# Key loads into five common buffers, four score buffers, four products ahead of their quads, and filler matmuls in the next operation's bank

## The chip, the cores and the metric

The kernel runs on one NeuronCore of a Trainium2 chip, in one launch. The metric is the device time of that core in microseconds, the median of several executions. Five engines run their own instruction streams and wait for each other through semaphores: TensorE (PE in the profile, its weight loads PEld), VectorE (DVE), ScalarE (ACT), GpSimd (POOL) and SyncE (SP), which here issues all DMA transfers.

## The reference

Attention over pooled keys and values, then a two-layer network with an unusual activation, all in fp32:

```python
# q, k, v: 8 batches x 8 heads x 576 positions x 64
k_p = k.reshape(B, H, Sp, pool, D).mean(axis=3)      # pool = 8, Sp = 72
v_p = v.reshape(B, H, Sp, pool, D).mean(axis=3)
scores = scale * np.matmul(q, k_p.transpose(0, 1, 3, 2))
attn = np.exp(scores - max); attn = attn / (sum + 1e-09)
x = np.matmul(attn, v_p)                             # as 4608 tokens x 512
h = x @ w_in                                         # 512 -> 2048
g = h * erf(softplus(h))
out = g @ w_out                                      # 2048 -> 512
```

## The kernel before

**Tiling.** The 4608 tokens are cut into nine chunks of 512. Chunk 0 goes through both matrix products directly (`plain_in`, then `second`). The other eight chunks are taken in four pairs. For a pair the first product is done by Strassen's scheme in Winograd's form: seven half-size products in place of eight. Sums and differences of the tokens' halves (`sides`: T1 to T4, B11 to B22) and of the weights' blocks (`sums`: S1 to S4) are made on DVE and POOL. Each fp32 operand is split into a high and a low part (`halves`; in the profile `x`, `w`, `ws`, `gl`), and a product is three matmuls for each 128 rows of the contraction (`three`), so that one product of the first layer is six matmuls of 128x512. The second layer of pairs 2 to 4 uses the same scheme (`seconds`), that of pair 1 doesn't.

**A quad.** `quad(s, i, ...)` makes eight of these per pair, each with the products S2·T2, S3·T3, S1·T1, A12·B21, A22·T4 and S4·B22, and A11·B11 unless that was made before. DVE adds them up as they come: v = p1 + S2T2, u = v + S3T3, g11 = u + S1T1, g00 = p1 + A12B21, then g10 and g01 (L831). A22·T4 accumulates onto the bank that S3·T3 used, so it can start only when u has been added; S4·B22 goes onto the bank of S1·T1 and needs g11. In pair 1 the first `HEADS = 7` quads have A11·B11 (p1) made ahead by `head`, between the second product of chunk 0 and the quads.

**The tokens come from attention.** `job` handles up to 256 positions of a batch. It loads keys and values (`load_pool`, a DMA each and one DVE reduction over 8), copies the pooled keys into `kbd`, then per tile of 128 positions: scores on PE (L579), maximum on DVE, exponentials on ACT (chunk 0: 8 instructions a tile with their sums, L598), normalisation, transposes on PE (L631, L634), values on PE (L674, L675), and x from the `att` banks. Keys land in `raw`, two buffers of their own of 128x576; the scores `s`, with their maxima `m` and sums `z`, have two buffers each, `bb` one.

**Who sets the order.** Every operation is recorded as an `Op` with a cost, a priority and the buffers that it holds. `Program.once` is a list scheduler over these with planned durations; `order` runs it eight times with new priorities and keeps the shortest plan. Each engine then executes its instructions in the planned order. A buffer kind has a number of places (`CAPS`), and most kinds share `PLACES` tiles of 128x512 in SBUF (`u`). The eight PSUM banks are shared by the kinds `h`, `o`, `att` and `cv`.

**Fillers.** Until the planned time `FILL` (57,000 ns) one bank is kept for filler matmuls (bf16, 128x256, on the constants; L998 in the profile): where the plan has PE idle ahead of an operation, as many of them are put there as fit into that idle time less `MARGIN`. After `FILL` there are none, and the bank goes to the other kinds.

Of the kernel before, what the change touches and what calls it, by code (L numbers as in the profile page):

```python
# [20 lines left out]
POOL = 8  # L21
# [4 lines left out]
P = 128  # L26
# [21 lines left out]
ON_DVE = 8  # L48
STORE = 6
HEADS = 7  # L50
EARLY, READY = (0, 0, 20, 32, 32), 14
ON_ACT = (0,)
CAPS = {"g": 32, "x": 28, "xr": 11, "w": 14, "ws": 10, "w0": 36, "gl": 12, "t": 6, "f": 3, "q": 2, "q0": 4, "f0": 14, "v": 3, "vm": 1, "low": 2, "sw": 8,
        "h": 6, "o": 4, "att": 4, "cv": 2, "dl": 3, "p1": 8}
SLACK, SLACK_SP, BIAS = 30, 400, 2000
FILL, MARGIN = 57000.0, 300
# [3 lines left out]
PLACES = 87  # L60
# [68 lines left out]
class Program:  # L129
# [100 lines left out]
    def once(self):  # L230
# [16 lines left out]
        spare = None  # L247
        if self.filler:
            spare = heapq.heappop(slots["bank"])
            self.idle.place = spare[1]  # L250
        for _ in self.ops:
# [100 lines left out]
def moe_attention(ctx: ExitStack, tc: tile.TileContext, cst, qa, kl, vl, wi, wo, out):  # L352
# [13 lines left out]
    sizes = {"u": PLACES, "bank": 8, "raw": 2, "et": 1, "etb": 1, "s": 2, "m": 2, "z": 2, "bb": 1, "ks": 1, "vs": 1, "d": 5}  # L366
# [148 lines left out]
    def job(ck, b, tiles, off, times, first, fresh):  # L515

        base, due, whole = times[0], times[-1] + VAL_R, ck > 2
        if fresh:
            ks, vs = buf("ks", [NP, SP]), buf("vs", [NP + 2, D])

            on_dve = b < ON_DVE

            def load_pool(src, dst, p, size, prio, tag):
                shape = [size, POOL] if on_dve else [POOL, size]
                t = buf("raw", shape) if tag == "raw" else place("v", F32, shape)
                op("SP", 15 * size, prio - 1, lambda: nc.sync.dma_start(
                    t.ap, src.rearrange("(p a b) -> p a b", p=P, b=t.ap.shape[2])), [], [t])
                if on_dve:
                    op("DVE", dve(8 * size), prio, lambda: nc.vector.tensor_reduce(  # L529
                        dst.ap[:, p, :], t.ap, AX.X, ALU.add), [t], [(dst, p)])  # L530
                else:
                    op("POOL", gps(4 * size), prio, lambda: nc.gpsimd.tensor_add(
                        t.ap[:, 0:4], t.ap[:, 0:4], t.ap[:, 4:8]), [t], [t])
                    op("POOL", gps(2 * size), prio, lambda: nc.gpsimd.tensor_add(
                        t.ap[:, 0:2], t.ap[:, 0:2], t.ap[:, 2:4]), [t], [t])
                    op("POOL", gps(size), prio, lambda: nc.gpsimd.tensor_add(
                        dst.ap[:, p, :], t.ap[:, 0], t.ap[:, 1]), [t], [(dst, p)])
# [7 lines left out]
            for p in range(NP + 2):  # L545
                load_pool(vl[b, p], vs, p, D, base + VALS + VALS_R * p,
                          "v")
# [263 lines left out]
    def quad(s, i, x, base, p1=None):  # L811
# [23 lines left out]
        g = {(m, t): place("g") for m in range(2) for t in range(2)}  # L835
# [161 lines left out]
    pr.idle = idle  # L997
    pr.filler = Op("PE", 107, 0, lambda: nc.tensor.matmul(  # L998
        idle.ap[:, :256], cb[:, :P], cb[:, :256], start=True, stop=True))
# [41 lines left out]
```

## Time and profile before

| | us |
|---|---|
| runs | 871.18, 877.29, 869.67 |
| median | 871.18 |
| the profiled execution | 870.09 |
| its span (first to last instruction) | 868.3 |
| granted TensorE clock, mean of the span | 0.996 |

The profiled execution lies 1.8 us above its own span and 1.1 us below the median. The profile names an instruction by line, engine, operation and the tiles it writes and reads (`h<-x,w` is a product of the first layer, `o<-gl,w` one of the second). In the timeline view a row is a run of equal instructions: start, duration from the first start to the last end, count, and in brackets the idle time of that engine before it with what ended it. In the windows view a row is a stretch of time with each engine's busy time, then the granted TensorE clock, the share of the DMA engines' time and the rate. Matmuls overlap, so six of them that take 1.52 us from first start to last end follow each other every 1.36 us.

### The profile page before, as it was taken

How to read it: one execution, taken by the hardware profiler on the slowest of the kernel's cores; microseconds unless marked ns; L12 is line 12 of the kernel's file. 1: busy time of each engine (PE TensorE's matmuls, PEld its weight loads, DVE VectorE, ACT ScalarE, POOL GpSimd, SP SyncE). 2: the span in 40 equal slices, each digit the busy share in tenths (PEclk: the TensorE clock that was granted, in tenths of full speed). 3: DMA queues.
4: the chain of work that ended last, by engine and by line, in shares of the span. 5: the costliest groups of instructions: out<-in, count | busy, mean ns of one | idle time of the engine just before them, and what ended most of it. 6: DMA issues, size and time to landing. Idle time of an engine off the chain costs nothing.

```text
span 868.3 us, 13644 instructions
## 1 busy us (share of the span) xinstructions
PE 850.9 (98%) x4134; PEld 702.7 (81%) x4134; DVE 698.6 (80%) x1272; ACT 574.4 (66%) x989; POOL 459.9 (53%) x482
## 2 busy tenths in 40 slices
PE   8999999799999999999999999999999999999998
PEld 7787788687888888888888888887887888888886
DVE  4987898989887888688798997877879975767872
ACT  4889877569884455478985642978866446777640
POOL 2888697567786774065557352564474323442310
PEclk9999999989999999999999999999999999999999
DMA  8899999997999899885285578924753679447541
GB/s 307 312 307 342 303 402 332 324 359 266 295 316 349 331 348 311 314 317 174 85 303 160 163 257 275 362 86 134 224 152 109 219 254 340 126 131 256 190 157 50
DMA packets 125208, 218.04 MB, mean 251 GB/s; under 512 B 16976, under 2 KB 31440, under 8 KB 125136
## 3 DMA queue, kind: packets, MB, share of 16 engines
q1 hardware_dynamic: 125136, 217.18, 72.6%
q8 instruction: 33, 0.54, 0.2%
q14 instruction: 39, 0.32, 0.1%
HBM read 167.84 MB, written 49.28 MB: 250 GB/s over the span
## 4 chain that ended last, share of the span: by engine, by line
PE 72%; DVE 2%; issue 0%; ACT 0%; DVEq 0%
PE o L746 36%; PE h L746 29%; PE att L579 3%; PE att L674 3%; PE att L631 1%; PE att L675 1%; DVE g L766 0%; DVE gl L411 0%; PE att L634 0%; DVE g L894 0%; DVE g L831 0%; DVE f L918 0%; DVE ks L529 0%; DVE t L831 0%; DVE s L624 0%
## 5 line engine op out<-in xcount | busy, mean ns | idle before, releaser
L746 PE MATMUL o<-gl,w 128*128 128x512 f32 x1584 | 377.1, 393 | 0.5 <-DVE g L769 0.3
L746 PEld LDWEIGHTS o<-gl,w 128*128 128x128 f32 x1584 | 292.7, 188 | 61.9 <-DVE gl L411 0.9
L746 PE MATMUL h<-x,w 128*128 128x512 f32 x1344 | 316.9, 392 | 2.0 <-DVE t L831 1.2
L746 PEld LDWEIGHTS h<-x,w 128*128 128x128 f32 x1344 | 249.7, 188 | 55.8 <-DVE t L831 2.5
L766 POOL TENSOR_TENSOR g<-d,g 128x512 f32<-128x512 f32 x68 | 90.7, 1351 | 98.7 <-ACT d L762 75.8
L399 ACT ACTIVATE gl<-g 128x512 fp32r<-128x512 f32 x185 | 109.3, 625 | 46.2 <-DVE g L894 20.2
L411 POOL TENSOR_TENSOR gl<-g,gl 128x512 fp32r<-128x512 f32 x67 | 100.0, 1501 | 66.8 <-ACT gl L399 32.4
L411 DVE TENSOR_TENSOR gl<-g,gl 128x512 fp32r<-128x512 f32 x149 | 110.2, 767 | 6.2 <-POOL gl L400 3.9
L831 DVE TENSOR_TENSOR g<-t,h 128x512 f32<-128x512 f32 x96 | 65.5, 684 | 31.6 <-PE h L746 29.9
L758 ACT ACT_TABLE_LOAD x48 | 61.6, 1283 | 20.7 <-PE h L746 20.0
L762 ACT ACTIVATE d<-d 128x1024 f32<-128x1024 f32 x72 | 73.7, 1054 | 0.4
L894 POOL TENSOR_TENSOR g<-g 128x512 f32<-128x512 f32 x36 | 51.8, 1439 | 25.0 <-DVE g L894 19.3
L758 ACT ACTIVATE d<-g 128x512 f32<-128x512 f32 x103 | 59.1, 623 | 5.6 <-DVE g L831 5.4
L831 DVE TENSOR_TENSOR t<-t,h 128x512 f32<-128x512 f32 x57 | 39.0, 685 | 27.8 <-PE h L746 26.1
L746 PE MATMUL h<-x,ws 128*128 128x512 f32 x192 | 48.4, 407 | 4.5 <-POOL sw L496 2.9
L762 ACT ACT_TABLE_LOAD x40 | 51.3, 1283 | 0.7
L399 ACT ACTIVATE x<-xr 128x512 fp32r<-128x512 f32 (+2 forms) x60 | 32.5, 563 | 28.9 <-DVE xr L720 21.5
L746 PEld LDWEIGHTS h<-x,ws 128*128 128x128 f32 x192 | 38.0, 199 | 13.1 <-POOL sw L496 3.0
L674 PE MATMUL att<-et,va 128*128 128x256 f32 (+3 forms) x192 | 45.5, 339 | 2.0 <-DVE s L604 1.4
L579 PE MATMUL att<-kbd,q 128*128 128x144 f32 (+1 forms) x320 | 45.9, 287 | 0.4 <-DVE x L694 0.4
L579 PEld LDWEIGHTS att<-kbd,q 128*128 128x128 f32 (+1 forms) x320 | 42.3, 179 | 5.0 <-issue 1.6
L642 ACT COPY et<-att 128x512 f32<-128x512 f32 (+1 forms) x40 | 21.8, 544 | 34.5 <-PE att L631 33.5
(91 smaller groups left out, 1145.3 us busy)
## 6 DMA issues: line engine op xcount, KB each, us to landing
w<-ws SPq DMA_DIRECT2D x192, 256.0 KB, 4.5
w<-wo SPq DMA_DIRECT2D x136, 256.0 KB, 3.6
w<-wi SPq DMA_DIRECT2D x96, 256.0 KB, 5.0
ws<-ws SPq DMA_DIRECT2D x64, 256.0 KB, 4.0
v<-vl SPq DMA_DIRECT2D x48, 256.0 KB, 5.7
raw<-kl SPq DMA_DIRECT2D x32, 288.0 KB, 4.5
out<-f SPq DMA_DIRECT2D x36, 256.0 KB, 2.0
q<-qa SPq DMA_DIRECT2D x32, 256.0 KB, 5.2
```

The source lines that it names most:

```text
L399: op("ACT", act(n), prio, lambda: nc.scalar.activation(dst(), src(), AF.Copy, scale=scale), *access, turn=turn, alt=("POOL", 0.833 * n + 1 ...
L411: both(True, dve(n), gps(n), prio + 0.1, lambda e: e.tensor_sub(lo(), src(), f32(hi())), reads + [hikey], [lokey])
L579: nc.tensor.matmul(o, raw.ap[:, p, :T], kbd[:, p], start=(p % 2 == 0), stop=True, skip_group_check=True)
L631: nc.tensor.transpose(pa.ap[:, P * p:P * p + T], sp[:, p, 0:P], ident[:T, :T])
L642: op("ACT", act(4 * T, True), r + 2.3, lambda: nc.scalar.copy(et.ap[:, :, cs], pav()), [pa], [(et, k)])
L674: nc.tensor.matmul(o, va[:, p], et.ap[:, p, :n], start=e == 0, stop=False, skip_group_check=True)
L746: nc.tensor.matmul(o, u, v, start=first and q == 0, stop=last and q == 2, skip_group_check=True)
L758: nc.scalar.activation(y(k), hs[k][0].ap, AF.Softplus)
L762: op("ACT", act(1024), prio + 0.2, lambda k=k: nc.scalar.activation(ys[k].ap, ys[k].ap, AF.Erf), own[2 * k:2 * k + 2], own[2 * k:2 * k + 2 ...
L766: both(True, dve(512), gps(512), prio + 0.3, lambda e, k=k, h=h: e.tensor_mul(h.ap, y(k), h.ap), [own[k], h], [h])
L831: op("DVE", dve(512), prio, lambda: nc.vector.tensor_add(dst.ap, u.ap, o.ap), [u, o], [dst])
L894: both(True, dve(512), gps(512), prio, lambda e: e.tensor_sub(out.ap, u.ap, v.ap), [u, v], [out])
```

## The change

**Keys.** `load_pool` is written anew. A batch's keys come as four blocks of 128x512 (64 of the 72 pooled positions of each head pair) and a fifth of 128x256 with the remaining 8 positions of all four pairs, and land in kind `k`: at most five of the common places, in place of the two `raw` buffers. That is 40 key transfers and 40 reductions in place of 32. The host lays keys and values out accordingly. All pooling was on DVE before (`ON_DVE` was 8 of 8 batches) and still is.

**Score buffers.** `s`, `m` and `z` have four buffers, `bb` has two. `PLACES` goes from 87 to 88, and an unused pad shrinks.

**Necks.** `neck` makes A12·B21 and its addition g00 = p1 + A12B21 for the first `NECKS = 4` quads of pair 1, after the heads. These quads then leave both out and take g00 as it is.

**Fillers.** No bank is kept. A filler writes the bank that the next operation takes anyway, so it stands only ahead of an operation that takes a new bank, and only from the planned time at which that bank is free. Besides the time until `FILL`, an idle time of more than `LONG_IDLE` (1,200 ns of the plan) is filled later too.

```diff
-ON_DVE = 8
-HEADS = 7
+HEADS, NECKS = 7, 4
-CAPS = {"g": 32, ..., "v": 3, "vm": 1, ...
+CAPS = {"g": 32, ..., "v": 3, "k": 5, "vm": 1, ...
-FILL, MARGIN = 57000.0, 300
+FILL, MARGIN, LONG_IDLE = 57000.0, 300, 1200.0
-PLACES = 87
+PLACES = 88
...
-        spare = None
-        if self.filler:
-            spare = heapq.heappop(slots["bank"])
-            self.idle.place = spare[1]
...
-            if spare is not None and o.eng == "PE":
-                if start > FILL:
-                    heapq.heappush(slots["bank"], (start, spare[1], None))
-                    spare = None
-                else:
-                    idle = start - max(free["PE"], 3000.0) - MARGIN - (1800 if not free["PE"] else 0)
-                    out.extend([self.filler] * int(idle / 107))
+            if o.eng == "PE":
+                new = [b for b in o.bufs if b.home == "bank" and not b.held]
+                idle = start - max(free["PE"], 3000.0) - (1800 if not free["PE"] else 0)
+                if new and (start < FILL or idle > LONG_IDLE):
+                    begin = max(free["PE"], 4800.0 if not free["PE"] else 0.0, slots["bank"][0][0])
+                    out.extend([(self.filler, new[0])] * int((start - begin - MARGIN) / 107))
...
-    sizes = {"u": PLACES, "bank": 8, "raw": 2, "et": 1, "etb": 1, "s": 2, "m": 2, "z": 2, "bb": 1, ...
+    sizes = {"u": PLACES, "bank": 8, "et": 1, "etb": 1, "s": 4, "m": 4, "z": 4, "bb": 2, ...
...
+            def load_pool(src, to, key, prio, kind, shape):
+                t = place(kind, F32, (*shape, POOL))
+                n = math.prod(shape)
+                names = "abcd"[:len(shape)]
+                op("SP", 15 * n, prio - 1, lambda: nc.sync.dma_start(
+                    t.ap.rearrange(f"p {' '.join(names)} e -> p ({' '.join(names)} e)"),
+                    src.rearrange("(p x) -> p x", p=P)), [], [t])
+                op("DVE", dve(8 * n), prio, lambda: nc.vector.tensor_reduce(to(), t.ap, AX.X, ALU.add), [t], [key])
+
+            n = P * D * POOL
             for p in range(NP):
-                load_pool(kl[b, p], ks, p, SP, base + KEYS + KEYS_R * p, "raw")
+                load_pool(kl[b, n * p:n * p + n], lambda p=p: ks.ap[:, p, :D], (ks, p),
+                          base + KEYS + KEYS_R * p, "k", (D,))
+            load_pool(kl[b, n * NP:], lambda: ks.ap[:, :, D:], (ks, NP), base + KEYS + KEYS_R * NP, "k", (NP, SP - D))
...
+    def neck(s, i, x, due, p1):
+
+        a12 = piece(lambda: in_hbm[i][:, 1], IN[i], due)
+        A, g = bank("h"), place("g")
+        product(A, a12, "B21", x, due, False, True)
+        op("DVE", dve(512), due + 0.3, lambda: nc.vector.tensor_add(g.ap, p1.ap, A.ap), [p1, A], [g])
+        return g
+
-    def quad(s, i, x, base, p1=None):
+    def quad(s, i, x, base, p1=None, g00=None):
...
-        if early:
+        if early and not g00:
             next(A, a12, "B21", False, True)
             add(g[0, 0], p1, A, due + 1.7)
         next(C, a22, "T4", True, True)
...
+        g00s = [neck(s, i, x, start(s) - 0.5, ps[i]) for i in range(NECKS if s == 1 else 0)]
         for i in range(NQ):
-            quad(s, i, x, start(s), ps[i] if i < len(ps) else None)
+            quad(s, i, x, start(s), ps[i] if i < len(ps) else None, g00s[i] if i < len(g00s) else None)
...
-    idle = bank("h")
...
+    pr.filler = lambda b: nc.tensor.matmul(b.ap[:, :256], cb[:, :P], cb[:, :256], start=True, stop=True)
```

Because the plan is made anew, the change also moves instructions that it doesn't touch. Three places follow, each before and after. Line numbers of the changed kernel are lower by 5 to 11 there (L735 is L746 of before, L663 is L674, L568 is L579, L805 and L829 are additions as L831 was, L995 is the filler).

The first place is SP at the very start: which transfers it issues in which order (`raw` and `k` are keys, `q` queries, `v` values, `d` the first layer's weights). Before:

```order
L415 DMA cst<-cst 128x136
L526 DMA raw<-kl 128x576 x2
L571 DMA q_215<-qa 128x512
L571 DMA q_217<-qa 128x512
L526 DMA v<-vl 128x512
L526 DMA raw<-kl 128x576 x2
L526 DMA v<-vl 128x512
L571 DMA q_232<-qa 128x512
```

And now:

```order
L409 DMA cst<-cst 128x136
L520 DMA k<-kl 128x512 x3
L560 DMA q_218<-qa 128x512
L520 DMA k<-kl 128x512
L520 DMA k<-kl 128x256
L560 DMA q_225<-qa 128x512
L520 DMA v<-vl 128x512 x2
L560 DMA q_237<-qa 128x512
```

The keys' last block is the sixth transfer after the constants where it was the seventh, and none of the five waits for a buffer; on ACT, the exponentials of chunk 0 come as runs of 20, 4, 4 and 4 now, and came as 16, 8 and 8.

The second place is PE where the quads of pair 1 begin, from 164.25 us of the trace before on (`h<-x,ws` is a product with S1 to S4, `h<-x,w` one with A11, A12 or A22; `att<-et,va` are the values of chunk 2's last tile). Before:

```order
L746 MATMUL h<-x,w 128x512 x12
L674 MATMUL att<-et,va 128x128
L675 MATMUL att<-etb,vb 64x128
L674 MATMUL att<-et,va 128x128
L675 MATMUL att<-etb,vb 64x128
L746 MATMUL h<-x,ws 128x512 x18
L746 MATMUL h<-x,w 128x512 x12
L746 MATMUL h<-x,ws 128x512 x24
```

Now, up to the first of the 52 fillers (each is a weight load and a matmul; the 51 others, alike, are left out), and then from the quads' first row on:

```order
L735 MATMUL h<-x,w 128x512 x18
L663 MATMUL att<-et,va 128x128
L664 MATMUL att<-etb,vb 64x128
L663 MATMUL att<-et,va 128x128
L664 MATMUL att<-etb,vb 64x128
L663 MATMUL att<-et,va 128x128
L664 MATMUL att<-etb,vb 64x128
L735 MATMUL h<-x,w 128x512 x18
L663 MATMUL att<-et,va 128x128
L664 MATMUL att<-etb,vb 64x128
L995 LDWEIGHTS cst
L995 MATMUL h<-cst 128x256
```

```order
L735 MATMUL h<-x,ws 128x512 x18
L735 MATMUL h<-x,w 128x512 x6
L735 MATMUL h<-x,ws 128x512 x24
L735 MATMUL h<-x,w 128x512 x6
L735 MATMUL h<-x,ws 128x512 x24
L735 MATMUL h<-x,w 128x512 x6
```

Three of the four necks stand ahead of the last value matmul, the fillers behind it, and in the first four quads the two products between S1·T1 and S4·B22 have become one.

The third place is DVE at the same point (`xr` are the sides before they are split, `x` their low parts; `x_2414` and `x_2450` before, `x_2443` and `x_2470` now are the low parts of T2, which S2·T2 reads). Before:

```order
L411 TENSOR_TENSOR x_2450<-xr_2432,x_2438 128x384
L411 TENSOR_TENSOR x_2414<-xr_2376,x_2385 128x128
L411 TENSOR_TENSOR x_2315<-xr_2289,x_2301 128x128
L720 TENSOR_TENSOR xr_2436<-xr_1426,xr_2376 128x128
L411 TENSOR_TENSOR x_2450<-xr_2432,x_2438 128x128
```

And now:

```order
L709 TENSOR_TENSOR xr_2483<-xr_1493,xr_2455 128x384
L709 TENSOR_TENSOR xr_2466<-xr_1495,xr_2421 128x128
L405 TENSOR_TENSOR x_2346<-xr_2149,x_2291 128x128
L805 TENSOR_TENSOR g_2491<-p1_2177,h_2409 128x512
L805 TENSOR_TENSOR g_2497<-p1_2238,h_2426 128x512
L805 TENSOR_TENSOR g_2503<-p1_2251,h_2446 128x512
L405 TENSOR_TENSOR x_2470<-xr_2455,x_2460 128x128
```

Three additions of the necks stand ahead of the last part of T2.

More of the change, by code (lines that the diff above doesn't have):

```diff
@@ L47 @@
 FIRST, LONG, SHORT, PERIOD = 17.5, 14.0, 20.5, 34.5
-ON_DVE = 8
 STORE = 6
-HEADS = 7
+HEADS, NECKS = 7, 4
 EARLY, READY = (0, 0, 20, 32, 32), 14
 ON_ACT = (0,)
-CAPS = {"g": 32, "x": 28, "xr": 11, "w": 14, "ws": 10, "w0": 36, "gl": 12, "t": 6, "f": 3, "q": 2, "q0": 4, "f0": 14, "v": 3, "vm": 1, "low": 2, "sw": 8,
+CAPS = {"g": 32, "x": 28, "xr": 11, "w": 14, "ws": 10, "w0": 36, "gl": 12, "t": 6, "f": 3, "q": 2, "q0": 4, "f0": 14, "v": 3, "k": 5, "vm": 1, "low": 2, "sw": 8,
         "h": 6, "o": 4, "att": 4, "cv": 2, "dl": 3, "p1": 8}
 SLACK, SLACK_SP, BIAS = 30, 400, 2000
-FILL, MARGIN = 57000.0, 300
+FILL, MARGIN, LONG_IDLE = 57000.0, 300, 1200.0
 DGE = 1200
@@ L365, in moe_attention @@
     hbm = pool("hbm", 1, space=bass.MemoryType.DRAM)
-    sizes = {"u": PLACES, "bank": 8, "raw": 2, "et": 1, "etb": 1, "s": 2, "m": 2, "z": 2, "bb": 1, "ks": 1, "vs": 1, "d": 5}
+    sizes = {"u": PLACES, "bank": 8, "et": 1, "etb": 1, "s": 4, "m": 4, "z": 4, "bb": 2, "ks": 1, "vs": 1, "d": 5}
     sizes.update(CAPS)
@@ L519, in job @@
             ks, vs = buf("ks", [NP, SP]), buf("vs", [NP + 2, D])
[L521 to L537, printed above, removed]
+            def load_pool(src, to, key, prio, kind, shape):
[7 more added lines that the diff above has]
+            n = P * D * POOL
             for p in range(NP):
-                load_pool(kl[b, p], ks, p, SP, base + KEYS + KEYS_R * p, "raw")
+                load_pool(kl[b, n * p:n * p + n], lambda p=p: ks.ap[:, p, :D], (ks, p),
+                          base + KEYS + KEYS_R * p, "k", (D,))
+            load_pool(kl[b, n * NP:], lambda: ks.ap[:, :, D:], (ks, NP), base + KEYS + KEYS_R * NP, "k", (NP, SP - D))
             for r0, c0 in ((64, 0), (0, SP)):
@@ L545, in job @@
             for p in range(NP + 2):
-                load_pool(vl[b, p], vs, p, D, base + VALS + VALS_R * p,
-                          "v")
+                load_pool(vl[b, n * p:n * p + n], lambda p=p: vs.ap[:, p, :], (vs, p),
+                          base + VALS + VALS_R * p, "v", (D,))
             for i in range(2):
@@ L819, in quad @@
         s2, s3, s1 = sm(1), sm(2), sm(0)
-        a12 = piece(lambda: in_hbm[i][:, 1], IN[i], due)
+        if g00 is None:
+            a12 = piece(lambda: in_hbm[i][:, 1], IN[i], due)
         a22 = piece(lambda: in_hbm[i + NQ][:, 1], IN[i + NQ], due)
         s4 = sm(3)
-        A, Bk, C, Dk = (bank("h") for _ in range(4))
+        A, Bk, C, Dk = (None if m == 0 and g00 else bank("h") for m in range(4))
         n = [0]
@@ L834, in quad @@
         fts = (i, i + NQ)
-        g = {(m, t): place("g") for m in range(2) for t in range(2)}
+        g = {(m, t): g00 if g00 and m + t == 0 else place("g") for m in range(2) for t in range(2)}
         if not early:
@@ L993, in moe_attention @@
             seconds(s, start(s) + LONG, span)
-    idle = bank("h")
     cb = c.bitcast(mybir.dt.bfloat16)
-    pr.idle = idle
-    pr.filler = Op("PE", 107, 0, lambda: nc.tensor.matmul(
-        idle.ap[:, :256], cb[:, :P], cb[:, :256], start=True, stop=True))
+    pr.filler = lambda b: nc.tensor.matmul(b.ap[:, :256], cb[:, :P], cb[:, :256], start=True, stop=True)
     ops = pr.order()
-    small.tile([P, 272], F32, tag="pad", name="pad")
+    small.tile([P, 176], F32, tag="pad", name="pad")
     for o in ops:
-        o.fn()
+        if isinstance(o, tuple):
+            o[0](o[1])
+        else:
+            o.fn()
 def kernel(q, k, v, moe_w_in, moe_w_out):
@@ L1022 @@
     vr = np.concatenate([va, np.concatenate([vb] * 4, axis=2)], axis=1)
-    kl, vl = (np.stack([(r[b].swapaxes(-1, -2) if b < ON_DVE else r[b]).reshape(r.shape[1], -1)
-                        for b in range(B)]) for r in (kr, vr))
+    kt = kr.swapaxes(-1, -2)
+    kl = np.concatenate([kt[..., :D, :].reshape(B, -1), kt[..., D:, :].transpose(0, 2, 1, 3, 4).reshape(B, -1)], axis=1)
+    vl = vr.swapaxes(-1, -2).reshape(B, -1)
     if moe_w_in.dtype.itemsize == 8:
```

## The prediction, made before the changed kernel ran

> **What bounds the kernel now.** I read the page first, then busy time by stage, then what PE waited for, then the timelines of the places where it waited.
>
> ```profile
> span 868.3 us, 13644 instructions
> PE 850.9 (98%) x4134; PEld 702.7 (81%) x4134; DVE 698.6 (80%) x1272; ACT 574.4 (66%) x989; POOL 459.9 (53%) x482
> ```
>
> ```profile
> 2.60:44.40 41.80, 39.28 (x297) 32.38 (x298) 32.17 (x75) 26.36 (x104) 22.43 (x30) 1.00 0.92 327
> 44.40:168.00 123.60, 120.92 (x603) 99.81 (x600) 105.45 (x206) 99.00 (x175) 95.44 (x114) 1.00 0.96 334
> ...
> 179.50:246.00 66.50, 65.29 (x285) 53.07 (x284) 58.70 (x88) 59.16 (x73) 52.49 (x61) 1.00 0.90 306
> 246.00:868.40 622.40, 618.18 (x2936) 511.86 (x2934) 492.62 (x879) 383.69 (x624) 282.76 (x271) 1.00 0.65 223
> ```
>
> PE is the first figure after the stretch's length. Behind 246 us it is idle for 4.2 of 622.4 us, most of that the end. Nothing that the change does can shorten those 622 us, since it removes no product. What can be gained lies ahead: the start, some small waits, and one stall near 170 us.
>
> ```profile
> PE h L746 <- POOL sw L496: 2.9, 1, 2.9
> PE h L746 <- DVE x L411: 1.6, 1, 1.6
> PE att L674 <- DVE s L604: 1.4, 1, 1.4
> PE h L746 <- DVE g L769: 0.8, 1, 0.8
> PE o L746 <- DVE g L769: 0.3, 1, 0.3
> ```
>
> The first two rows are the stall; the other three (2.5 us) lie between 72 and 95 us.
>
> **Term 1, the start.** These rows are the timeline of PE (two), DVE (four), ACT (one) and SP (two).
>
> ```profile
> 2.69 9.56 PE L998 MATMUL h<-cst 128*128 128x256 bf16 x62 [2.69 <-DMA cst<-cst]
> 12.09 2.13 PE L579 MATMUL att<-kbd,q 128*128 128x144 f32 x16
> 7.28 0.69 DVE L529 TENSOR_REDUCE vs<-v 128x64 f32<-128x512 f32 x1 [1.36 <-DMA v<-vl]
> 10.10 0.75 DVE L529 TENSOR_REDUCE ks<-raw 128x72 f32<-128x576 f32 x1 [1.11 <-DMA raw<-kl]
> 13.73 0.81 DVE L588 TENSOR_REDUCE m<-att 128x4 f32<-128x288 f32 x2
> 44.81 0.41 DVE L694 TENSOR_TENSOR x<-att,x 128x256 fp32r<-128x256 f32 x1
> 10.95 0.87 ACT L543 COPY kbd<-ks 64x288 f32<-64x288 f32 x2 [8.72 <-DVE ks L529]
> 1.19 0.90 SPq L526 DMA_DIRECT2D raw<-kl  x2
> 4.84 1.44 SPq L526 DMA_DIRECT2D raw<-kl  x2
> ```
>
> The third and fourth key blocks were issued only at 4.84, when the first had been reduced, and the last was there at 10.10. Now the last key block stands sixth after the constants, where the first values stood, and those were there at 7.28 with slightly fewer bytes ahead; so 7.4. One small reduction and the copies of 0.87 put `kbd` at about 8.7 in place of 11.8: 3.1 us. Ahead of the scores stand 45 fillers now in place of 62. These windows (fillers alone) show the first 25 in the 5.3 us to 8.00 and the other 38 in the 4.2 us behind that, one straddling:
>
> ```profile
> 2.00:8.00 6.00, 5.30 (x25) 3.76 (x26) 1.00 0.98 302
> 8.00:12.20 4.20, 4.20 (x38) 3.57 (x36) 1.00 0.89 271
> ```
>
> So 45 fillers end at 8.0 + 20 × 0.11 = 10.2, and it is they that hold the scores: 2.0 us earlier than 12.09, not 3.1. The maxima follow at about 10.9 to 11.7 (before: 1.6 us after the scores began, some of it behind a reduction of values). From there I go by DVE. Before, it was nearly without a pause from 13.73 to the last low part of x at 45.2 (44.81 + 0.41): 31.5 us. Counted by the order, with each form's mean duration of before, DVE has 31.5 us of work between these two points before and 32.3 now (a scaling of s and two masks came over from POOL; one weight less is converted). That gives 10.9 + 32.3 = 43.2 to 44.0 for the last x. The value matmuls are now spread among 16, 14, 14 and 15 fillers and the first product follows the last 15, so it starts roughly 1 us ahead of the last x, as it did before.
>
> ```profile
> 44.48 27.46 PE L746 MATMUL h<-x,w 128*128 128x512 f32 x120
> ```
>
> I take 43.2 in place of 44.48: minus 1.3 us. Bounds: DVE's pauses in that stretch (about 3.3 us) also vanish, minus 4.5; or the four score tiles queue behind each other and it starts as late as before, plus 0.5. Four buffers take the waits out of the scores, but DVE was full, and full it stays: this is why I don't book the 5 us that ACT's unbroken run of exponentials seems to promise.
>
> Edits at no cost: eight more key transfers are SP issues of 0.45 us each (0.90 for two, above), and SP was waiting there. Eight more reductions are smaller ones: 32 × 0.741 = 23.7 us become 32 × 0.66 + 8 × 0.34 = 23.8, in proportion to their size, on DVE, which carries them under PE's products; without that cover they would cost 0.1 us.
>
> ```profile
> L529 DVE TENSOR_REDUCE ks<-raw 128x72 f32<-128x576 f32 x32 | 23.3, 741 | 5.9 <-DMA raw<-kl 5.8
> ```
>
> **Term 2, the small waits.** Of the 2.5 us between 72 and 95 us I take half as gone, minus 1.2: the value matmuls that waited 1.4 us for s now stand behind more second-layer products, and the plan around them is another one. Bounds: all gone, minus 2.5; or as much new waiting, plus 2.5, since PE arrives 1 to 3 us earlier while DMA is at 0.96.
>
> **Term 3, the stall.**
>
> ```profile
> 167.45 0.30 PE L675 MATMUL att<-etb,vb 96*64 96x128 f32 x1
> 170.63 0.47 PE L746 MATMUL h<-x,ws 128*128 128x512 f32 x1 [2.88 <-POOL sw L496]
> 172.72 6.95 PE L746 MATMUL h<-x,ws 128*128 128x512 f32 x17 [1.62 <-DVE x L411]
> 179.51 2.89 PE L746 MATMUL h<-x,w 128*128 128x512 f32 x12
> 190.40 5.60 PE L746 MATMUL h<-x,ws 128*128 128x512 f32 x24
> 195.84 1.52 PE L746 MATMUL h<-x,w 128*128 128x512 f32 x6
> ```
>
> ```profile
> 167.70:172.70 5.00, 0.52 (x2) 0.19 (x1) 4.74 (x12) 3.17 (x12) 2.82 (x4) 0.92 1.04 344
> 172.70:179.50 6.80, 6.78 (x17) 5.35 (x18) 5.01 (x16) 1.86 (x6) 3.45 (x1) 0.56 1.02 338
> ```
>
> After the last values PE waits for the low part of T2, and then runs at a granted clock of 0.56. From 167.75 to 179.51 it does 18 matmuls, which at full clock take 18 × 0.227 (5.44 us for 24) = 4.1 us: the stall costs 7.7 us, 4.5 in waits and the rest in clock.
>
> The four necks move 4 × 1.36 = 5.4 us of products from behind this point to ahead of it. That alone changes no sum. Their additions (0.675 us each, row below) move along. But in the new order the necks don't fill the stall: three stand ahead of the last value matmul, and the stall is filled by 52 fillers, 52 × 0.114 = 5.9 us (0.114 from this row).
>
> ```profile
> 31.62 4.32 PE L998 MATMUL h<-cst 128*128 128x256 bf16 x38
> ```
>
> PE executes them whether it needs them or not, so the stall costs at least 5.9 us, and with the clock kept, no more, if T2 is there by then. From the last values T2 needs an ACT copy, a difference, an ACT rounding and a DVE difference of 0.3 to 0.5 us each, and 4.1 us of necks and 5.9 of fillers cover the earlier parts. So 5.9 against 7.7: minus 1.8 us. Bounds: 0 if waiting and half clock come on top of some of it; worse is a rival.
>
> [...]
>
> **Term 4, the cover that the necks take away.** A22·T4 waits for u, and A12·B21 stood between. These are DVE (two rows) and PE (two) in the second and third quad.
>
> ```profile
> 187.23 0.68 DVE L831 TENSOR_TENSOR t<-t,h 128x512 f32<-128x512 f32 x1
> 196.84 0.67 DVE L831 TENSOR_TENSOR t<-t,h 128x512 f32<-128x512 f32 x1
> 187.68 2.88 PE L746 MATMUL h<-x,w 128*128 128x512 f32 x12
> 197.56 1.65 PE L746 MATMUL h<-x,w 128*128 128x512 f32 x6 [0.20 <-DVE t L831]
> ```
>
> Without A12·B21, A22·T4 could start at 187.68 and 195.84; u ended at 187.91 and 197.51. With DVE unchanged the second quad would wait 0.25 us and the third 1.4 more than now: 1.65 together. The first and fourth had u in time. Now v and u stand next to each other on DVE in these quads, with four additions and some splitting done earlier, so I take 0.5. Bounds: 0, and 5.4, where DVE and ACT pace the quads (58.70 and 59.16 busy of 66.5) and nothing that was moved ahead is gained.
>
> **Sum.** −1.3 − 1.2 − 1.8 + 0.5 = −3.8 us on the profiled execution's 870.09: 866.3 (a span of 864.5). The median of the runs stands 1.1 above that execution; I don't add it. A difference under 1% of 871.18 can hardly be told from no change; these bounds are 862.5 and 879.9.
>
> **Rivals.** *Everything comes through.* DVE's pauses at the start vanish (−4.5), all small waits go (−2.5), no cover is missed, the stall as above (−1.8): −8.8, so 861.3. For it: four buffers do take out real waits. Against: DVE's 32 us of work.
>
> *DVE delivers T2 late: slower.* Up to the last part of T2 DVE has some 9 us more work ahead than before, by the order: four necks' additions (2.7), three more scalings of s (2.8), five more weight sums (2.8) and others.
>
> ```profile
> L831 DVE TENSOR_TENSOR g<-p,h 128x512 f32<-128x512 f32 x7 | 4.7, 675 | 0.3 <-PE h L746 0.3
> L624 DVE TENSOR_TENSOR s<-s,z 128x576 f32<-128x576 f32 x24 | 22.3, 930 | 2.1 <-POOL bb L620 1.8
> L497 DVE TENSOR_TENSOR sw<-sw 128x256 f32<-128x256 f32 x6 | 3.4, 560 | 0.0
> ```
>
> DVE has 123.6 − 105.45 = 18 us of idle time to take it in. If it takes in none, T2 comes 9 − 1.3 later than at 172.7, near 180.5, and PE, with its necks and fillers done at about 176, waits 4.5 us and falls to half clock again (3.2 us, as above): −3.8 + 7.7 = +3.9, so 874.0. It decides once DVE takes in less than half of the 9 us. [...]
>
> *It does nothing.* The start is paced by fillers and DVE, and the quads by DVE and ACT as in the upper bound of term 4: −1.3 − 1.8 + 3 = 0, so 870.
>
> **How the numbers follow.** My forecast 0.55 (863 to 869.5), everything comes through 0.17, T2 late 0.15, nothing 0.13. Faster by over 1% is most of the first rival and a little of the forecast's lower end: 0.15. Slower by over 1% needs T2 late and the lost cover together: 0.05. The rest, 0.80, is within 1%. The range runs from just under the first rival to T2 late: 860.5 to 874.
>
> **What would show it.** In the profile after: scores from about 10.2, the first product of the first layer near 43.2 (under 41: the first rival), 52 fillers in one row near 170 and behind them a wait under 0.5 us and a clock of 1.00 to 190 us (a wait for x there and a clock near 0.6: T2 late), waits for DVE's t in the first four quads under 1 us in sum. A new wait behind 246 us would make the whole account wrong.

## The result, and the profile after

The changed kernel takes 863.1 us (median of 20 runs, 859.02 to 868.86), the kernel before 871.19 us (median of 20, 868.53 to 877.46). The ratio is 0.9897 with a 95% interval of 0.9874 to 0.9920: 1.0% faster, just at the bound of 1% that I had set. The median lies where no run is: ten runs lie between 859.0 and 860.5 us (median 859.3), ten between 865.7 and 868.9, none between. The profiled execution (868.86 us, span 867.0) is one of the upper group. The kernel before spreads too: six of its 20 runs lie above 873 us, and no trace of one of those was taken.

The stages after, from the windows view of the changed kernel (PE, PEld, DVE, ACT, POOL busy, granted clock, DMA share, rate):

```profile
2.60:44.40 41.80, 39.33 (x277) 31.85 (x278) 35.78 (x85) 28.75 (x107) 21.65 (x28) 1.00 0.98 351
44.40:168.00 123.60, 122.51 (x611) 100.96 (x609) 108.25 (x214) 97.55 (x177) 97.58 (x116) 1.00 0.98 350
168.00:179.50 11.50, 11.39 (x79) 9.49 (x77) 10.00 (x21) 5.19 (x13) 5.81 (x11) 1.00 1.02 361
179.50:246.00 66.50, 61.32 (x256) 49.95 (x257) 53.03 (x74) 54.86 (x68) 48.80 (x54) 0.95 0.80 262
246.00:867.00 621.00, 617.21 (x2934) 511.67 (x2932) 497.48 (x888) 392.60 (x640) 267.76 (x259) 1.00 0.66 223
```

PE is nearly always busy up to 179.5 us and behind 246 us. The stage in between, that of the first pair's quads, is idle for 5.2 us at a granted clock of 0.95; before, it was idle for 1.2 us there. Next, what PE waited for in the changed kernel (the five longest):

```profile
PE h L735 <- DVE t L829: 5.2, 1, 5.2
PE att L995 <- DMA cst<-cst: 2.8, 1, 2.8
PE att L623 <- POOL bb L609: 1.3, 1, 1.3
PE att L568 <- ACT kbd L532: 0.6, 1, 0.6
PE att L664 <- POOL etb L640: 0.6, 1, 0.6
```

One wait is left, and it is new. These rows are PE's timeline at the start, at the place of the old stall, and at the new wait:

```profile
10.54 2.13 PE L568 MATMUL att<-kbd,q 128*128 128x144 f32 x16
40.30 10.01 PE L735 MATMUL h<-x,w 128*128 128x512 f32 x43
167.93 0.30 PE L664 MATMUL att<-etb,vb 96*64 96x128 f32 x1
168.08 5.85 PE L995 MATMUL h<-cst 128*128 128x256 bf16 x52
173.69 4.35 PE L735 MATMUL h<-x,ws 128*128 128x512 f32 x18
204.18 2.93 PE L735 MATMUL h<-x,w 128*128 128x512 f32 x6 [5.17 <-DVE t L829]
206.91 7.08 PE L735 MATMUL h<-x,ws 128*128 128x512 f32 x24
```

The first product starts at 40.30 (before: 44.48). The quads follow the 52 fillers at once and at a granted clock of 1.00. In the fourth quad A22·T4 waits 5.17 us for u, and the next 30 matmuls take 2.93 and 7.08 us in place of 1.52 and 5.60: with the clock, granted at 0.50 from 204.0 to 209.5 us, that is 8.1 us lost. The same moment on DVE (first four rows) and on POOL (the others):

```profile
194.96 0.69 DVE L829 TENSOR_TENSOR g<-t,h 128x512 f32<-128x512 f32 x1
195.56 7.17 DVE L405 TENSOR_TENSOR gl<-g,gl 128x512 fp32r<-128x512 f32 x1
202.66 0.67 DVE L829 TENSOR_TENSOR t<-p,h 128x512 f32<-128x512 f32 x1
203.44 0.69 DVE L829 TENSOR_TENSOR t<-t,h 128x512 f32<-128x512 f32 x1
...
195.28 2.57 POOL L755 TENSOR_TENSOR g<-d,g 128x512 f32<-128x512 f32 x2
197.79 1.46 POOL L405 TENSOR_TENSOR ws<-sw,ws 128x256 fp32r<-128x256 f32 x2
199.18 0.75 POOL L490 TENSOR_TENSOR sw<-sw 128x256 f32<-128x256 f32 x1
199.86 1.28 POOL L755 TENSOR_TENSOR g<-d,g 128x512 f32<-128x512 f32 x1
201.08 0.75 POOL L492 TENSOR_TENSOR sw<-sw 128x256 f32<-128x256 f32 x1
201.78 0.43 POOL L394 TENSOR_SCALAR ws<-sw 128x256 fp32r<-128x256 f32 x1
202.82 0.41 POOL L394 TENSOR_SCALAR ws<-sw 128x256 fp32r<-128x256 f32 x1 [0.62 <-DVE gl L405]
```

A subtraction of 128x512 takes 7.17 us, where one of the same form at 491.47 us of the execution "again" (below) takes 0.68. Its row shows no idle time ahead of it, so the profile puts none of the 7.17 us down to a wait for another engine's result. All the while GpSimd runs eight instructions without a pause, seven of them with two operands in SBUF, as this subtraction has. It ends only when GpSimd itself has to stop, 0.62 us, for this very subtraction. The eighth instruction is also the one of the row with a single operand, so this trace can't tell whether VectorE was let in by it or by the pause. Behind it stand v and u of the fourth quad, for which PE waits; PE does not need the subtraction's own result before 216 us.

Other rows of this trace show a shorter hold-up; these are one of DVE and, at the same moment, two of POOL:

```profile
127.56 1.78 DVE L405 TENSOR_TENSOR gl<-g,gl 128x512 fp32r<-128x512 f32 x1
...
127.04 1.75 POOL L405 TENSOR_TENSOR w<-f,w 128x512 fp32r<-128x512 f32 x1
128.75 1.19 POOL L491 TENSOR_TENSOR sw<-sw 128x256 f32<-128x256 f32 x1
```

VectorE's subtraction takes 1.78 us and ends 0.55 us behind the first GpSimd instruction (129.34 and 128.79), as if held to its end, and GpSimd's next one, of 128x256, takes 1.19 us, where rows of that form take 0.75 at 199.18 and 201.08. The subtraction at 195.56 was held for all eight.

### The profile page after: what moved, and what is told of

Its sections match the earlier page's. It is cut to its first block, busy times and chain, and to the rows that moved or that the text cites. A ratio compares the mean times of both kernels' runs of the same rounds, so it can differ in the third digit from the quotient of the medians.

```text
span 867.0 us, 13697 instructions
## 1 busy us (share of the span) xinstructions
PE 851.8 (98%) x4151; PEld 703.9 (81%) x4151; DVE 704.5 (81%) x1278; ACT 580.4 (67%) x1004; POOL 442.4 (51%) x471
## 4 chain that ended last, share of the span: by engine, by line
PE 85%; DMA 5%; DVE 3%; POOL 2%; ACT 2%; SPq 2%; issue 1%; DVEq 0%; ACTq 0%; POOLq 0%
PE o L735 40%; PE h L735 35%; PE att L568 4%; PE att L663 3%; PE att L620 2%; DMA v<-vl 1%; DMA q<-qa 1%; DMA wf<-f 1%; PE att L664 1%; DVE gl L405 1%; DMA d<-wi 1%; POOL gl L405 1%; DMA wi<-w 1%; POOL w L405 0%; SPq L520 0%
## 5 line engine op out<-in xcount | busy, mean ns | idle before, releaser
L735 PE MATMUL o<-gl,w 128*128 128x512 f32 x1584 | 374.7, 393 | 0.0
L735 PEld LDWEIGHTS o<-gl,w 128*128 128x128 f32 x1584 | 293.4, 188 | 60.9 <-issue 0.4
L735 PE MATMUL h<-x,w 128*128 128x512 f32 x1344 | 317.7, 393 | 5.2 <-DVE t L829 5.2
L735 PEld LDWEIGHTS h<-x,w 128*128 128x128 f32 x1344 | 250.5, 188 | 58.2 <-DVE t L829 5.6
L405 POOL TENSOR_TENSOR gl<-g,gl 128x512 fp32r<-128x512 f32 x69 | 97.5, 1422 | 44.7 <-ACT gl L393 37.3
L405 DVE TENSOR_TENSOR gl<-g,gl 128x512 fp32r<-128x512 f32 x147 | 114.5, 802 | 4.4 <-ACT gl L393 4.3
L829 DVE TENSOR_TENSOR g<-t,h 128x512 f32<-128x512 f32 x96 | 65.5, 684 | 30.0 <-PE h L735 28.4
L892 POOL TENSOR_TENSOR g<-g 128x512 f32<-128x512 f32 x37 | 57.3, 1551 | 39.2 <-PE o L735 18.0
L829 DVE TENSOR_TENSOR t<-t,h 128x512 f32<-128x512 f32 x57 | 39.0, 684 | 23.5 <-PE h L735 22.4
L393 ACT ACTIVATE x<-xr 128x512 fp32r<-128x512 f32 (+2 forms) x56 | 30.4, 564 | 27.3 <-DVE xr L709 21.4
L609 POOL TENSOR_TENSOR bb<-s,z 128x64 f32<-128x64 f32 (+1 forms) x40 | 13.1, 330 | 68.6 <-DVE z L603 41.1
L568 PE MATMUL att<-kbd,q 128*128 128x144 f32 (+1 forms) x320 | 47.0, 288 | 0.6 <-ACT kbd L532 0.6
L735 PE MATMUL h<-x,ws 128*128 128x512 f32 x192 | 47.0, 400 | 0.1
L568 PEld LDWEIGHTS att<-kbd,q 128*128 128x128 f32 (+1 forms) x320 | 42.1, 179 | 6.0 <-issue 2.8
L892 DVE TENSOR_TENSOR g<-g 128x512 f32<-128x512 f32 x59 | 45.3, 773 | 0.7
L663 PE MATMUL att<-et,va 128*128 128x256 f32 (+3 forms) x192 | 45.5, 340 | 0.2 <-ACT et L631 0.2
```

The source lines that it names most:

```text
L393: op("ACT", act(n), prio, lambda: nc.scalar.activation(dst(), src(), AF.Copy, scale=scale), *access, turn=turn, alt=("POOL", 0.833 * n + 1 ...
L405: both(True, dve(n), gps(n), prio + 0.1, lambda e: e.tensor_sub(lo(), src(), f32(hi())), reads + [hikey], [lokey])
L568: nc.tensor.matmul(o, raw.ap[:, p, :T], kbd[:, p], start=(p % 2 == 0), stop=True, skip_group_check=True)
L609: nc.gpsimd.tensor_mul(bb.ap[:T], sv, zv.unsqueeze(2).broadcast_to([T, NP, 16]))
L663: nc.tensor.matmul(o, va[:, p], et.ap[:, p, :n], start=e == 0, stop=False, skip_group_check=True)
L735: nc.tensor.matmul(o, u, v, start=first and q == 0, stop=last and q == 2, skip_group_check=True)
```

## The experiments

All are variants of the changed kernel unless they say otherwise; the ratio is to the kernel before in runs on the same chip.

| kernel | median us (range, runs) | ratio [95%] |
|---|---|---|
| again | 863.40 (859.52–867.47, 6) | 0.9908 [0.9874, 0.9943] |
| low_later | 860.88 (860.24–861.74, 5) | 0.9879 [0.9852, 0.9905] |
| pool_gap | 859.87 (859.55–860.39, 5) | 0.9868 [0.9845, 0.9891] |
| pool_read | 860.51 (860.03–860.86, 6) | 0.9865 [0.9838, 0.9893] |
| pool_early | 860.83 (860.24–866.29, 6) | 0.9879 [0.9841, 0.9917] |
| two_scores | 872.99 (869.97–874.50, 10) | 1.0009 [0.9987, 1.0031] |
| four_only | 868.67 (867.09–869.87, 10) | 0.9951 [0.9928, 0.9974] |
| old_keys | 863.81 (863.56–865.72, 6) | 0.9899 [0.9864, 0.9934] |
| no_necks | 863.98 (862.86–866.14, 6) | 0.9907 [0.9878, 0.9936] |
| necks_7 | 859.13 (857.91–860.20, 6) | 0.9842 [0.9811, 0.9874] |
| no_late | 860.81 (859.79–862.39, 6) | 0.9871 [0.9840, 0.9902] |
| both_cut | 860.17 (859.30–860.84, 6) | 0.9862 [0.9834, 0.9889] |

### What parts the two groups

**The changed kernel again.** No edit.

> The changed kernel once more, to see its two groups of times in one trace more. Its 20 runs fell into two groups of ten, 859.0 to 860.5 and 865.7 to 868.9 us, and the profiled one is of the upper group. [...]

Three of six runs lie at 865.1 to 867.5, three at 859.5 to 861.7. The profile is of the lower group (859.76 us). Its timeline of DVE and of POOL at the same place:

```profile
194.03 0.69 DVE L829 TENSOR_TENSOR g<-t,h 128x512 f32<-128x512 f32 x1
194.63 0.99 DVE L405 TENSOR_TENSOR gl<-g,gl 128x512 fp32r<-128x512 f32 x1
195.55 0.67 DVE L829 TENSOR_TENSOR t<-p,h 128x512 f32<-128x512 f32 x1
...
193.77 3.02 POOL L755 TENSOR_TENSOR g<-d,g 128x512 f32<-128x512 f32 x2
```

Here the subtraction takes 0.99 us, and GpSimd's pair is held instead (3.02 us in place of 2.57). Setting the starts of PE's products side by side in the order of work, the lower execution leads the upper one by 0.4 us at the first product, by 0.9 ahead of this place, by 9.1 behind it, and by 9.1 to the end. So some 8.2 of the 9.1 us arise here, and a cause that is spread over the whole execution is out. PE's row for the product that began at 204.18 there:

```profile
197.93 1.52 PE L735 MATMUL h<-x,w 128*128 128x512 f32 x6
```

**The subtraction moved** behind the next eight instructions of DVE, once the plan is made:

```diff
+    dve_ops = [o for o in ops if not isinstance(o, tuple) and o.eng == "DVE"]
+    low = [o for o in dve_ops if sum(b.name == "gl" for b in o.bufs) == 2][1]
+    behind = dve_ops[dve_ops.index(low) + 8]
+    ops.remove(low)
+    ops.insert(ops.index(behind) + 1, low)
```

> The changed kernel with that one VectorE subtraction (a low part for the second layer, not needed by PE before some 216 us) moved behind the next eight VectorE instructions, so that the additions for which PE waits in the fourth quad are ahead of it. Nothing else is moved and nothing left out. Theory (the held-up subtraction makes the upper group): nearly all runs between 858.5 and 861, median near 859.3, no wait of PE over 1.5 us between 180 and 250 us. Rival one: it strikes the next VectorE instruction with two operands in SBUF instead; then still about half of the runs are above 865. Rival two (a spread cause): half of the runs above 865 as before.

Five runs of five between 860.2 and 861.8: the upper group is gone. The median is 1.6 us above the lower group's 859.3. In its profile PE waits 1.3 us more for `bb` in the softmax than in that of "again" (2.6 us in two waits); the added wait stands at 83.6 us, far ahead of what was moved.

**A gap in GpSimd's row.** Three memsets between its instructions, VectorE's order untouched:

```diff
+    pool_ops = [o for o in ops if not isinstance(o, tuple) and o.eng == "POOL"]
+    for o in pool_ops[168:171]:
+        ops.insert(ops.index(o) + 1, (lambda p: nc.gpsimd.memset(p[:, :8], 0.0), pad))
```

> The changed kernel with three memsets of 128x8 put into GpSimd's stream, each behind one of the three additions and products that ran while VectorE's subtraction was held up; VectorE's order is as in the changed kernel. Nothing is left out. [...]

All five runs between 859.55 and 860.39. DVE and POOL in its profile:

```profile
194.65 1.41 DVE L405 TENSOR_TENSOR gl<-g,gl 128x512 fp32r<-128x512 f32 x1
...
194.21 1.30 POOL L755 TENSOR_TENSOR g<-d,g 128x512 f32<-128x512 f32 x1
195.44 0.11 POOL L1001 MEMSET pad<- 128x8 f32 x1
195.50 1.72 POOL L755 TENSOR_TENSOR g<-d,g 128x512 f32<-128x512 f32 x1
```

VectorE gets in at the first memset: 1.41 us in place of 7.17. It did so between these two additions in "again" too, where nothing stood there, so it is the five runs that count, not this profile. Whether a memset lets it in because it reads nothing, the next run asks.

**Small copies in the memsets' place:** they read SBUF and take 0.2 us.

```diff
-nc.gpsimd.memset(p[:, :8], 0.0)
+nc.gpsimd.tensor_scalar(out=p[:, 8:16], in0=p[:, :8], scalar1=1.0, scalar2=0.0, op0=ALU.mult, op1=ALU.add)
```

> As the kernel with three memsets in GpSimd's stream (859.55 to 860.39 in all five runs, the subtraction 1.41 us), but each memset of 128x8 is now a small copy that reads and writes 128x8 of SBUF. It shifts GpSimd's later instructions by about as much (0.1 us each) but leaves no gap in its reading. One more memset of 128x8 at the very start sets up what is read. Theory one (a gap in GpSimd's reading lets VectorE in): some runs are held up again, near 865 to 868, about half of them as in the changed kernel (3 of 6 at 865.1 to 867.5). Theory two (any small instruction or the shift of 0.1 us is enough): all runs between 859 and 861.

All six runs between 860.0 and 860.9, so theory one is wrong: no gap in the reading is needed. **The same memsets ahead of the row** then tell a mere shift apart:

```diff
-    for o in pool_ops[168:171]:
+    for o in pool_ops[160:163]:
```

> The changed kernel with the same three memsets of 128x8 in GpSimd's stream, but eight instructions earlier, ahead of the unbroken row of GpSimd instructions during which VectorE's subtraction is held up. The row itself is as in the changed kernel, only some 0.2 to 0.3 us later. Theory one (what lets VectorE in is an instruction without two operands in SBUF between GpSimd's additions): some of the runs, about half, are held up again and lie between 864 and 869. Theory two (the hold-up hangs on the exact time between the two engines, and a shift of 0.2 us is enough to miss it): all runs at 859 to 861, as with the memsets or the small copies inside the row. Theory three: the shift meets it always, all runs above 864.

Two of six runs are held up (865.93, 866.29), the others lie at 860.2 to 861.2. So this shift alone does not do it. With a small instruction within the row, 0 of 11 runs were above 861 us, and two kernels further below that have the memsets too had 0 of 12 above 862.4; without one, 15 of 32 were above 865 (the 20 runs of the result, 6 of "again", 6 here). What in the chip decides between 0.99 and 7.17 us stays open. The moment of arrival alone does not: the subtraction came 0.28 us after GpSimd's addition began in the execution that was held up, and 0.29 us after it in the profile of the small copies (194.71 and 194.42), where it took 1.55 us; in that of these memsets it took 1.61.

### What the parts are worth

**Two score buffers again.**

```diff
-"s": 4, "m": 4, "z": 4, "bb": 2,
+"s": 2, "m": 2, "z": 2, "bb": 1,
```

> The changed kernel with two buffers for scores, maxima and sums and one for the ends, as before; everything else as changed. The plan is made anew, so this is read at the start. In the changed kernel the first product of the first layer begins at 40.3 us (before: 44.48), 2.9 us earlier than I predicted from VectorE's work. Theory one: the four buffers did this, by taking VectorE's pauses in the softmax away: with two the first product begins at 42.5 to 44.5 us. Theory two: the keys and the fillers did it, and the buffers are worth nothing there: 40.3 to 41.2 us. Time by theory one: lower group near 862, by theory two near 859.5.

The first product begins at 43.42 us, so at the start theory one holds. The whole gain is gone, though, and I had foreseen 3 us of it: the profiled execution (874.50 us, the slowest of ten) has long waits of PE elsewhere, of which these two lie between 85 and 200 us (what PE waited for, this kernel):

```profile
PE att L995 <- DVE s L593: 2.4, 1, 2.4
PE att L568 <- DVE f L452: 2.4, 1, 2.4
```

The second of them, at 126 us, is a hold-up of the same kind at another place. These rows are one of DVE and, at the same time, three of POOL:

```profile
118.43 5.37 DVE L405 TENSOR_TENSOR gl<-g,gl 128x512 fp32r<-128x512 f32 x1
...
118.12 1.39 POOL L613 TENSOR_TENSOR s<-s,z 64x576 f32<-64x576 f32 x1
119.48 2.51 POOL L405 TENSOR_TENSOR w<-f,w 128x512 fp32r<-128x512 f32 x2
121.96 1.28 POOL L405 TENSOR_TENSOR gl<-g,gl 128x512 fp32r<-128x512 f32 x1
```

The subtraction is held for four GpSimd instructions of two operands. So the time of this kernel is not the price of the buffers alone; how many of its ten runs were held up is not known.

**Four score buffers alone** (an edit of the kernel before):

```diff
-"s": 2, "m": 2, "z": 2, "bb": 1,
+"s": 4, "m": 4, "z": 4, "bb": 2,
-PLACES = 87
+PLACES = 86
```

> The kernel before, with four buffers for scores, maxima and sums and two for the ends, and nothing else of the change; one common place less (86), so that it fits. The plan is made anew. Each part left out of the changed kernel alone cost much: 13.7 us for the buffers (872.99 against 859.3), 4.5 for the keys (863.81), 4.7 for the necks (863.98), which is 22.9 us in sum where the whole change is worth 11.9. Theory one (the parts help each other: the buffers bring their worth only where the keys no longer wait): 868 to 872, the first product of the first layer at 43 to 44.5 us. Theory two (the buffers alone carry most of it): 862 to 866, the first product at 41 to 42.5.

0.5% faster, some 4 us, with the first product at 42.39. The time is that of theory one, the start that of theory two: the buffers shorten the start by 2.1 us by themselves. That they need the other parts for the rest fits, but each of these kernels is also planned anew, which the runs don't part from it.

**The old keys.**

```diff
-                          base + KEYS + KEYS_R * p, "k", (D,))
-            load_pool(kl[b, n * NP:], lambda: ks.ap[:, :, D:], (ks, NP), ...)
+                load_pool(kl[b, p], lambda p=p: ks.ap[:, p, :], (ks, p), base + KEYS + KEYS_R * p, "raw", (SP,))
...
-PLACES = 88
+PLACES = 86
```

> The changed kernel with the keys as before: four blocks of 128x576 a batch into two buffers of their own, 86 common places; score buffers, necks and fillers as changed. The plan is made anew and has no memsets, so compare the lower runs with 859.3 and read the start. My prediction gave the keys 3.1 us at the start of the scores, of which fillers hid 1.1. Theory one (the keys let the scores start earlier, and the first product follows): scores at 11.8 to 12.2 us in place of 10.1 to 10.5, first product 41.5 to 42.5 in place of 39.9 to 40.3, lower runs near 861. Theory two (VectorE's work takes the delay up again): scores at 12, first product at 39.9 to 40.8, lower runs at 859 to 860.

Scores at 12.20 and the first product at 43.26, later than both theories had it: the delay is not taken up again, it grows: the new plan has 29.4 us of VectorE's work between the first maximum and the last low part of x, where the changed kernel has 28.1. The time is 863.81, 4.5 us above the changed kernel's lower group, 3 to 3.4 of them at the start.

**No necks, and seven.** Without necks all quads have A12·B21 again, and the plan is made anew:

```diff
-HEADS, NECKS = 7, 4
+HEADS, NECKS = 7, 0
```

> [...] Theory one (as predicted: four products of 1.36 us moved from behind the stall to ahead of it change no sum; the fillers, the buffers and the keys brought what was gained): 859 to 861, and the first quad starts some 5 us earlier than in the changed kernel, at 167 to 169 us. Theory two (T2 is late by the work of VectorE, ScalarE and GpSimd, not by the last values on PE, so the necks fill a wait that is there anyway): the first quad starts at 171 to 173 us as now, and the time is 862.5 to 865.

863.98, a time within theory two. PE's timeline without necks:

```profile
162.80 7.93 PE L995 MATMUL h<-cst 128*128 128x256 bf16 x71
170.48 4.37 PE L735 MATMUL h<-x,ws 128*128 128x512 f32 x18
```

The last values end at 162.8 us, 4.3 us earlier than in "again", but the first quad starts only 2.3 us earlier than there (172.75), between what the two theories had: the plan fills the wait for T2 with 71 fillers in place of 52. The necks had taken the place of fillers. Their four products, 5.4 us, are still to do in the quads, which leaves 3.1 us; at the end the profiles differ by 4.3. With seven:

```diff
-HEADS, NECKS = 7, 4
+HEADS, NECKS = 7, 7
```

> The changed kernel with seven necks in place of four. Nothing else is changed; the plan is made anew and puts 29 fillers where 52 stood ahead of the first quad. Without necks the time was 863.98, with four 859.3 in the lower runs, so a neck is worth some 1.1 us so far. Theory one (T2 comes late by the work of the other engines, and every product moved ahead of it takes the place of fillers): 23 fillers less are 2.6 us: 856.5 to 857.5 in the lower runs. Theory two (the seven additions and the seven loads of A12 delay T2 on VectorE, or the quads miss their cover): PE waits for x behind the fillers or for t in the quads, 859 to 862. [...]

859.13, and none of six runs held up. The fillers shrink to 29; by PE's products the kernel leads "again" by 1.8 us in the first quads and has lost it by 237 us. For the lower group that is theory two.

**Fewer fillers**, on top of the memsets:

```diff
-FILL, MARGIN, LONG_IDLE = 57000.0, 300, 1200.0
+FILL, MARGIN, LONG_IDLE = 57000.0, 300, 1e9
```

> The kernel with the three memsets, and without the 52 fillers ahead of the first quad. Nothing else moves. In that kernel the last values end at 166.8 us, the last low part of T2 at 171.1 and the first product of the quads starts at 172.3, so the fillers cost 1.2 us of waiting. Theory one (without them the clock falls to half as before the change): PE waits 4.3 us, starts at 171.1 and then loses some 3 us at a granted clock near 0.56: 861 to 862, which is 1.3 to 2 us slower than 859.9. Theory two (the clock stays at 1.00): 858.5 to 859. Theory three: the next product's operands come later than 172.3 and the 52 fillers cost nothing: the same start and half clock on top, 862.5 or more.

PE's timeline and one row of its windows without the 52 fillers:

```profile
167.74 0.91 PE L735 MATMUL h<-x,ws 128*128 128x512 f32 x3
171.62 5.70 PE L735 MATMUL h<-x,ws 128*128 128x512 f32 x15 [2.97 <-ACT x L393]
...
171.80:180.00 8.20, 8.06 (x28) 0.79 1.03 353
```

Three matmuls of S2·T2 are done early, the wait is 2.97 us, and the granted clock is 0.79 over the 8.2 us behind it (15 matmuls in 5.70 us, at full clock 3.4). The ratio, 0.9871, can't be told from 0.9868 with the fillers, nor 860.81 us from the 860.51 of the small copies, which have the fillers and ran on the same chip: they cost what they save. Cutting 12 fillers at the start and 12 here, with the memsets too, gave nothing either:

```diff
+    fill = [i for i, o in enumerate(ops) if isinstance(o, tuple)]
+    for i in reversed(fill[:12] + fill[-12:]):
+        del ops[i]
```

> The kernel with the three memsets, with 12 fewer fillers at the start (33 in place of 45 ahead of the scores) and 12 fewer ahead of the first quad (40 in place of 52). The block of keys is ready at 9.40 us there and the scores start at 9.72 behind the fillers; 33 fillers end by some 8.7. [...] The first quad starts 1.1 to 1.2 us earlier if T2 is then there (171.1 against 172.3). Together minus 1.4 to 1.9: 858.0 to 858.5. Rival: PE waits for what GpSimd and VectorE make for the next product, and the second part gives nothing: 859.3 to 859.9. [...]

The scores started at 10.36 us, no earlier than with 45 fillers (9.72 to 10.65 in the profiles with the changed keys), because the keys' last blocks came late in this execution (PE waited 2.61 us for `kbd`); at the quads PE then waited 1.00 us for an addition. The forecast's 1.4 to 1.9 us, less 1.1 to 1.2 at the first quad, leave 0.3 to 0.7 for the scores: 0.3 is what lay between the keys at 9.40 and the scores at 9.72, the 0.7 no run shows, and neither came. 0.9862 is no gain over 0.9868.

The kernels with a small instruction within the row (0.9862 to 0.9871) and that with seven necks (0.9842) were never held up, and lie below the changed kernel's 0.9897. Only the interval of seven necks (up to 0.9874) ends where that of the changed kernel begins; the others overlap with it, and with each other, so which is best isn't settled.

## Why the prediction was right, and where it was not

The forecast was 866.3 with a range of 860.5 to 874.0 and most of the chance on less than 1%; 863.1 lies within the range, and the ratio of 0.9897 at that bound of 1%. But this was luck: it was right by the median of two groups, with errors of opposite sign, and no single run did what it says: the lower group, 859.3, is faster than the rival in which everything comes through (861.3), and the upper group is slowed by something that was in no rival. The terms, by the profile of "again" (859.76, 10.3 us below the execution before), each measured where PE does the same product:

| term | predicted | measured |
|---|---|---|
| start | −1.3 (−4.5 to +0.5) | −4.6 |
| small waits | −1.2 | −1.3 |
| stall near 170 us | −1.8 | −1.8 |
| lost cover in the quads | +0.5 (0 to +5.4) | −1.8; in the upper group +6.4 |
| behind 246 us | 0 | −0.7 |

**The start** was the worst step, with the quads. "Counted by the order, with each form's mean duration of before, DVE has 31.5 us of work" took durations for time. Instructions of DVE overlap: in the rows of "again" above, one starts 0.60 us after the other and lasts 0.69. The busy time of the same stretch, from the first maximum to the last low part of x, is in the windows of DVE before, after and in "again":

```profile
13.73:45.21 31.48, 27.99 (x71) 1.00 0.90 334
...
11.24:40.45 29.21, 28.11 (x71) 1.00 0.97 357
...
10.84:40.05 29.21, 28.11 (x71) 1.00 1.00 364
```

DVE had 28.0 us of work and 3.5 of pauses, and now has 28.1 and 1.1. Of the 5.2 us by which the stretch ends earlier in "again", 2.9 come from the first maximum (10.9 predicted, 10.84 measured) and 2.3 from the stretch itself, for which I had 0.8 more. "DVE was full, and full it stays" was false, and the bound of −4.5 that I had noted for just that was the outcome. That the score buffers removed most of the pauses is shown by the same stretch of the two runs that change them alone, four buffers in the kernel before and two in the changed one:

```profile
13.69:43.38 29.69, 28.10 (x72) 1.00 0.83 279
...
11.34:43.97 32.63, 30.57 (x74) 1.00 0.82 301
```

Four leave 1.6 us of pauses where there were 3.5; two leave 2.1 where there were 1.1, and the new plan puts 2.5 us more work there. The fillers were read rightly: scores at 10.2 predicted, 10.54 and 10.14 measured.

**The stall** was right in size and its reason half right. In the profile after, the fillers take 5.85 us (predicted 5.9), T2's last part ends at 172.50, 1.2 us ahead of their end, and the granted clock is 1.00 from 168.00 to 179.50. That fillers would keep it there was my assumption in that term; without the 52 it was 0.79 in the mean of the 8.2 us from 171.80 on. But "that alone changes no sum", on the necks, was wrong: without them the plan needs 71 fillers, and the time is 4.3 us longer by the profiles. The fillers, to which I gave the gain, are worth nothing that can be measured: without them PE waits 2.97 us for T2, where it waited 4.5 before.

**Lost cover** did not show: in "again" PE waits for no t in the quads, and the 1.2 us that it waited for them before are gone; the rest of the 1.8 was not traced. In "With DVE unchanged the second quad would wait" the condition did not hold, since DVE now adds u as PE delivers. The rival of a late T2, which I gave 0.15, did not happen in any profile of the changed kernel: DVE took its additional work in. One sum of the rivals doesn't follow, though it didn't carry the forecast: "as in the upper bound of term 4" is 5.4, where the sum takes 3.

**The hold-up** of VectorE by GpSimd was missing. I looked for the place where DVE has too much work, and not for the one where an instruction of two SBUF operands stands right ahead of additions for which PE waits, beside an unbroken row of GpSimd. The order of the changed kernel shows both; that this costs some 8 us in half of the executions could not be read from the profile before, whose longest such VectorE instruction takes 1.83 us. The other side of it could: a GpSimd subtraction at 816.41 us takes 5.05 us there, beside a row of VectorE instructions 0.60 us apart.

## What to carry to other kernels

Take an engine's work in a stretch from its busy time there, not from a sum of durations: with some 70 short instructions the sum was 4 us too high, and it hid the pauses that the change removed. Run a changed kernel many times and look at the single times before reading its one profile; here two groups with nothing between them came from one place, and a second profile found it. Where VectorE works for a waiting PE, look for an instruction of it with two SBUF operands beside an unbroken row of such instructions on GpSimd: here one took 7.17 us in place of 0.68, and no run was held up once it was moved away (0 of 5) or a short instruction stood in the row (0 of 11). What parts of a change cost when left out singly need not add up: here it was 13.7 (with a hold-up of its own in it), 4.5 and 4.7 us, of a change that is worth 11.9 in its lower group.

## What the hardware showed beyond that

GpSimd is held up by VectorE in the same way and for longer. In "again", far from any wait of PE, an addition took 9.06 us, of a kind that takes 1.30 us in the median on GpSimd (L892 in the changed kernel's profile), while thirteen VectorE instructions ran 0.60 us apart; it ended at 502.34, behind a pause of VectorE of 0.93 us. In the upper execution it took 1.74 us, with 1.78 us for each of three VectorE instructions: there the engines took turns. So here too the same order has two outcomes. The rows are POOL's, then the last of DVE's before the pause and the first behind it:

```profile
493.28 9.06 POOL L892 TENSOR_TENSOR g<-g 128x512 f32<-128x512 f32 x1
...
500.50 0.68 DVE L892 TENSOR_TENSOR g<-g 128x512 f32<-128x512 f32 x1
502.10 1.37 DVE L916 TENSOR_TENSOR f<-t,o 128x512 f32<-128x512 f32 x2 [0.93 <-PE o L735]
```
